# Layer 1 of an MLP by Strassen's scheme on blocks of 512 tokens, and square sums in the exponential's bias

## The chip, the cores and the metric

The kernel runs on one core of a Trainium2 chip, as one launch with one instruction list for each engine: PE (TensorE), ACT (ScalarE), DVE (VectorE), POOL (GpSimd) and SP (SyncE, which issues all DMAs). The metric is the device time of one execution in microseconds.

## The reference

```python
# attention, batch 8, 8 heads, 576 tokens, head size 64, 128 random features
scale = 1 / sqrt(sqrt(64))
def phi(x):
    proj = x @ omega.T                          # 128 features
    sq = sum(x * x, axis=-1) / 2
    h = proj - sq
    return exp(h - max(h)) / sqrt(128)
q_p, k_p = phi(q * scale), phi(k * scale)
num = q_p @ (k_p.T @ v);  den = q_p @ sum(k_p) + 1e-6
x = num / den                                   # 4608 tokens x 512
# MLP, w_in 512 x 2048, w_out 2048 x 512
h = x @ w_in
g = where(h > 0, h, exp(min(h, 0)) - 1)
out = g @ w_out
```

The weights come in float64. They are converted on the chip, from their 64-bit words.

## The kernel before

**Precision.** A matmul of the MLP is made of three passes in fp32r, high x high, high x low and low x high. Each operand is split into a rounded high part (a cast) and a low part (a subtraction).

**Attention.** A pair is two heads of one batch entry; there are 32 pairs, four to a batch. `load_pair`, `project` (k and q), `kv` and `finish` emit a pair's work. Of the first pairs (7 for k, 8 for q, `NNAT`) the projection runs natively in fp32, with the squares as extra rows of the matmul. For the others x is split into high and low in one tile (`tk`, `tq`), a matmul of 256 columns gives two parts in PSUM (`pp`), ACT copies the second part with the square sum as its bias and a scale of -1 (`rest`, line 497, one instruction per 128 rows), DVE subtracts it and takes the maximum (line 506), ACT negates the maximum (`negate`, line 410), and ACT takes the exponential (line 404). `finish` divides, transposes and multiplies; its result goes as high and low parts into rings of two batches of tokens, `xh` and `xl`.

**MLP.** Twelve blocks of 384 tokens, 16 steps each; a step is one 128-column slice f of w_in and the same rows of w_out. `layer1` makes 4 x 3 matmuls of 384 columns into a PSUM bank `ph` (two of them in turn, lines 764 to 766). The tile goes through ACT (Relu of -h, Exp, lines 773 and 774), DVE (line 777, which reads `e` in SBUF and `ph` in PSUM), a cast to the high part of `g` (line 333) and a subtraction for its low part (line 336, POOL or DVE). `layer2` makes 3 x 3 matmuls of 512 columns into three banks `acc` (lines 798 to 800).

**Weights.** `from_f64` converts a 128 x 512 chunk: two ACT passes, then on DVE a clamp (697, sometimes POOL), a shift (704) and a merge (709), then an integer addition on POOL (712), a cast to the high part, a subtraction to the low part on POOL (336). There are 32 chunks, 16 of each matrix. w_out stays in SBUF (`w2h`, `w2l`). w_in goes to a scratch buffer `w1s` in DRAM and is fetched again, 512 KB a step, into `w1c` (three buffers). Blocks 0 to 2 run in halves: first slices 0 to 7 of blocks 0, 1 and 2, then slices 8 to 15, with the first halves' sums parked in DRAM (`part`). A slice is converted ahead of its step of block 0, so the second eight are due while blocks 1 and 2 run their first halves.

**Order.** Nothing is scheduled on the chip. `Plan` takes each operation with an engine, a cost in ns, a due time, reads and writes, plays them through a model of engines, buffers and latencies, and writes each engine's list in the order it finds. Some operations name a second engine (`alt`, table `ALT`). On the chip each engine runs its list in order and waits on semaphores. Batch 0 comes ahead of the MLP, batch 1 beside block 0, and batches 2 to 7 beside blocks 2, 3, 5, 6, 8 and 9.

## Time and profile before

| | |
|---|---|
| three runs | 1092.15, 1090.98, 1088.34 us; median 1090.98 |
| profiled execution, span of its instructions | 1090.7 us (no other time of that execution is listed) |
| busy, share of the span | PE 97%, PEld 86%, ACT 66%, DVE 58%, POOL 37% |
| chain that ended last | PE 79%, DVE 9%, ACT 6%, issue 3% |
| layer 1 matmuls (764 to 766), busy | 787.0 us in 2304, modelled ends that overlap |
| layer 2 matmuls (798 to 800), busy | 686.5 us in 1728 |
| HBM | 155.48 MB read, 20.19 MB written |

How to read it: a matmul's record runs to a modelled end, so records overlap and a group's busy time is more than its share of the span; the distance from start to start is what a matmul costs in a stream. The granted clock of PE is given as a share of full speed. On DVE, ACT and POOL a record runs to the acknowledged write. A record's length includes time in which the engine holds the instruction and can't go on.

### The profile page before, as it was taken

How to read it: one execution, taken by the hardware profiler on the slowest of the kernel's cores; microseconds unless marked ns; L12 is line 12 of the kernel's file. 1: busy time of each engine (PE TensorE's matmuls, PEld its weight loads, DVE VectorE, ACT ScalarE, POOL GpSimd, SP SyncE). 2: the span in 40 equal slices, each digit the busy share in tenths (PEclk: the TensorE clock that was granted, in tenths of full speed). 3: DMA queues.
4: the chain of work that ended last, by engine and by line, in shares of the span. 5: the costliest groups of instructions: out<-in, count | busy, mean ns of one | idle time of the engine just before them, and what ended most of it. 6: DMA issues, size and time to landing. Idle time of an engine off the chain costs nothing.

```text
span 1090.7 us, 19072 instructions
## 1 busy us (share of the span) xinstructions
PE 1060.6 (97%) x5971; PEld 936.8 (86%) x5971; DVE 635.9 (58%) x2403; ACT 724.7 (66%) x2027; POOL 404.4 (37%) x372
## 2 busy tenths in 40 slices
...
GB/s 213 171 181 161 208 188 240 218 186 205 207 205 130 169 170 150 165 118 157 176 155 153 193 139 170 162 119 150 162 155 167 157 164 79 117 164 119 161 121 63
DMA packets 53235, 176.90 MB, mean 162 GB/s; under 512 B 6032, under 2 KB 6224, under 8 KB 53136
## 3 DMA queue, kind: packets, MB, share of 16 engines
...
q14 instruction: 51, 0.42, 0.1%
HBM read 155.48 MB, written 20.19 MB: 161 GB/s over the span
## 4 chain that ended last, share of the span: by engine, by line
PE 79%; DVE 9%; ACT 6%; issue 3%; DMA 1%; POOL 1%; SPq 0%; DVEq 0%; POOLq 0%; ACTq 0%
PE ph L764 11%; PE acc L798 10%; PE acc L800 10%; PE ph L766 10%; PE acc L799 10%; PE ph L765 10%; PE pkv L535 4%; PE ppq L488 3%; PE pn L634 3%; PE pt L607 2%; PE ppk L488 2%; ACT hk L404 1%; DVE u_w L697 1%; DVE u_w L704 1%; DVE u_w L709 1%
## 5 line engine op out<-in xcount | busy, mean ns | idle before, releaser
L336 POOL TENSOR_TENSOR g<-e,g 128x384 fp32r<-128x384 f32 x182 | 189.2, 1040 | 547.7 <-DVE g L333 405.9
L764 PE MATMUL ph<-xh,w1c 128*128 128x384 f32 x768 | 267.5, 348 | 6.7 <-DVE e L777 6.2
L766 PE MATMUL ph<-xh,w1c 128*128 128x384 f32 x768 | 259.8, 338 | 0.0
L765 PE MATMUL ph<-xl,w1c 128*128 128x384 f32 x768 | 259.7, 338 | 0.0
L777 DVE SCALAR_TENSOR_TENSOR e<-e,ph 128x384 f32<-128x384 f32 x192 | 105.9, 552 | 237.2 <-ACT e L774 232.8
L798 PE MATMUL acc<-w2h,g 128*128 128x512 f32 x576 | 231.4, 402 | 0.0
L773 ACT ACTIVATE e<-ph 128x384 f32<-128x384 f32 x192 | 93.6, 488 | 206.4 <-PE ph L766 198.4
L800 PE MATMUL acc<-w2h,g 128*128 128x512 f32 x576 | 227.7, 395 | 0.0
L799 PE MATMUL acc<-w2l,g 128*128 128x512 f32 x576 | 227.4, 395 | 0.0
L764 PEld LDWEIGHTS ph<-xh,w1c 128*128 128x128 f32 x768 | 145.6, 190 | 20.1 <-DVE e L777 8.5
L765 PEld LDWEIGHTS ph<-xl,w1c 128*128 128x128 f32 x768 | 145.8, 190 | 7.2
L766 PEld LDWEIGHTS ph<-xh,w1c 128*128 128x128 f32 x768 | 145.4, 189 | 0.3 <-POOL w1c L336 0.3
L800 PEld LDWEIGHTS acc<-w2h,g 128*128 128x128 f32 x576 | 108.5, 188 | 25.5
L798 PEld LDWEIGHTS acc<-w2h,g 128*128 128x128 f32 x576 | 108.7, 189 | 15.1 <-issue 2.3
L799 PEld LDWEIGHTS acc<-w2l,g 128*128 128x128 f32 x576 | 108.8, 189 | 12.2
L336 POOL TENSOR_TENSOR hq<-hq,den 128x512 f32<-128x512 f32 (+1 forms) x96 | 90.4, 961 | 36.1 <-DVE den L595 24.6
L774 ACT ACTIVATE e<-e 128x384 f32<-128x384 f32 x192 | 100.7, 525 | 3.1
L333 DVE CAST g<-e 128x384 fp32r<-128x384 f32 x166 | 72.8, 439 | 23.5 <-PE acc L800 18.8
L586 DVE CUSTOM_DVE_ANT_0 junk<-hq,pz 128x128 f32<-128x128 f32 (+1 forms) x320 | 74.1, 279 | 16.9 <-PE pz L570 16.1
L506 DVE CUSTOM_DVE_ANT_0 hq<-ppq,p2q 128x128 f32<-128x128 f32 x216 | 54.3, 287 | 41.8 <-ACT p2q L497 40.2
L506 DVE CUSTOM_DVE_ANT_0 hk<-ppk,p2k 128x128 f32<-128x128 f32 x225 | 56.5, 286 | 36.1 <-ACT p2k L497 34.3
L497 ACT ACTIVATE p2q<-ppq,sqq 128x128 f32<-128x128 f32 x216 | 67.8, 367 | 12.5 <-PE ppq L488 10.8
...
## 6 DMA issues: line engine op xcount, KB each, us to landing
w1c<-w1s SPq DMA_DIRECT2D x176, 512.0 KB, 3.3
...
```

Source lines behind the costliest of these rows:

```text
L336: (nc.vector if e == "DVE" else nc.gpsimd).tensor_tensor(*args)
L506: nc.vector.tensor_tensor_reduce(out=h()[:, j, :], in0=view()[:, a, 0:M], in1=p2()[:, a, :], scale=1.0, scalar=LOWEST, op0=ALU.subtract, o ...
L586: nc.vector.tensor_tensor_reduce(out=junk()[r], in0=h()[r, j, :], in1=pz()[r, a * P:(a + 1) * P], scale=1.0, scalar=EPS, op0=ALU.mult, op1 ...
L764: nc.tensor.matmul(ph(), wh, xh[:, c, o:o + TB], start=(c == 0), stop=False)
L765: nc.tensor.matmul(ph(), wh, xl[:, c, o:o + TB], start=False, stop=False)
L766: nc.tensor.matmul(ph(), wl, xh[:, c, o:o + TB], start=False, stop=(c == NC - 1))
L773: op("ACT", act(TB, True), due, lambda: nc.scalar.activation(e(), ph(), AF.Relu, scale=-1.0), (p,), (e,))
L774: op("ACT", act(TB), due + 0.2, lambda: nc.scalar.activation(e(), e(), AF.Exp, scale=-1.0), (e,), (e,))
L777: lambda: nc.vector.scalar_tensor_tensor(e(), e(), -1.0, ph(), ALU.add, ALU.max), (p, e), (e,),
L798: nc.tensor.matmul(a(), g()[:, 0, ts], w2h[:, f], start=(f == f0), stop=False)
L799: nc.tensor.matmul(a(), g()[:, 0, ts], w2l[:, f], start=False, stop=False)
L800: nc.tensor.matmul(a(), g()[:, 1, ts], w2h[:, f], start=False, stop=(f == f1 - 1))
```

## The change

Layer 1 now takes nine blocks of 512 tokens and pairs of slices (8 steps j a block, e = 0 or 1 in a pair). Features (two halves), tokens (two halves T of 256) and slices (two) form 2 x 2 blocks, and one level of Strassen's scheme in Winograd's form gives the four results from seven products of half size: a product is 2 x 3 matmuls of 256 columns. The x sides (`units`: x11, x21, x22 and four sums, split into high and low, `xo`) are made once a block, the weight sides (`convert`: four sums, seven pieces `w1p`, split) once in block 0, written to `w1s` and fetched in each later block, 256 KB a piece. Products 0, 5, 6 and 3 add up in one bank A, with a copy to SBUF between them (`save`); products 1, 4 and 2 go to one bank B, from which DVE forms three of the four results in SBUF (`total`, `h`). So `e` is now made from `h` in SBUF for three tiles of four. Halved blocks and `part` are gone: all weights are converted within block 0. Batch s+1 of attention runs beside block s, s = 0 to 6. PSUM: four banks `acc`, A, B, and two shared ones `pa` (before: three `acc`, two `ph`, three `pa`). Attention's result is kept once, unsplit, in `xs`. In the projection, the second part is copied without bias, 256 columns at a time, DVE adds instead of subtracting, and the square sum goes into the exponential's bias by two small DVE operations (`bias`) instead of `rest` and `negate`. The model's price of a matmul changes from n/2.4 + 2.5 to n/2.2 + 1 ns.

```diff
-TB = 384
-NTT = TB // P
-NBLK = NTOK // TB
+SB = 512
+TH = SB // 2
+NTT = SB // P
+NSB = NTOK // SB
+NJP = NF // 2
+NPROD = 7
...
+NLARGE = 6
+NPIECE, NUNIT, NU, NXT, NRAW, NHS, NG = 7, 7, 3, 3, 3, 4, 5
+
+
+MLP0 = 56.0
+STEP0, STEP_ATT, STEP = 16.0, 13.3, 10.8
...
-SPLIT = (0, 8, 16)
-NHALF = 3
...
+ORDER = (0, 1, 5, 4, 6, 3, 2)
+L1_AT = {0: 0.0, 1: 0.08, 5: 0.2, 4: 0.28, 6: 0.36, 3: 0.52, 2: 0.6}
+LAG2 = 0.75
...
-    w1s = dram.tile([NF, P, 2 * NC * P], F32, name="w1s")
-    part = dram.tile([3 * TB, DM], F32, name="part")
-    xh = const.tile([P, NC, RING], F32R, name="xh")
-    xl = const.tile([P, NC, RING], F32R, name="xl")
+    w1s = dram.tile([NJP * NPROD, P, 4 * P], F32, name="w1s")
+    xs = const.tile([P, NC, RING], F32, name="xs")
...
+        return Buf(ps, [P, 512], F32, tag, name, dict(pa=2).get(tag, 1))
...
+        def bias(g, js, due):
+            def f():
+                nc.vector.scalar_tensor_tensor(mx()[:, js], mx()[:, js], SCALE, sq()[:, js], ALU.mult, ALU.subtract)
+                nc.vector.scalar_tensor_tensor(nb()[:, js], mx()[:, js], -1.0, sq()[:, js], ALU.mult, ALU.subtract)
+
+            op("DVE", 2 * dve(4), due, f, ((mx, g), sq), ((mx, g), (nb, g)))
+
+        y = large([P, 2 * S], F32R, f"t{nm}_{i}")
...
-            def rest(c=c, n=n, p2=p2, view=view):
-                for a in range(n):
-                    j = 2 * c + a
-                    nc.scalar.activation(
-                        p2()[:, a], view()[:, a, M:], AF.Identity, bias=sq()[:, j:j + 1], scale=-1.0
-                    )
-
-            op("ACT", n * act(M, True, True), d + 0.5, rest, (p, sq), (p2,))
+            op(
+                "ACT", act(n * M, True), d + 0.5,
+                lambda e, n=n, p2=p2, view=view: copy(e, p2()[:, 0:n], view()[:, 0:n, M:]), (p,), (p2,),
+                alt=other("part", "DVE", dve(n * M)),
+            )
 
             def ttr(c=c, n=n, p2=p2, view=view):
                 for a in range(n):
                     j = 2 * c + a
                     nc.vector.tensor_tensor_reduce(
                         out=h()[:, j, :], in0=view()[:, a, 0:M], in1=p2()[:, a, :], scale=1.0, scalar=LOWEST,
-                        op0=ALU.subtract, op1=ALU.max, accum_out=mx()[:, j:j + 1],
+                        op0=ALU.add, op1=ALU.max, accum_out=mx()[:, j:j + 1],
...
+            o = qs.start + (b % 2) * S
+            op(
+                "ACT", act(n, True), d + 0.8 + half, lambda e, o=o, n=n, p=p: copy(e, xs[:, hp, o:o + n], p()[:, 0:n]),
+                (p,), [("xs", hp, z) for z in range(o // D, (o + n) // D)], alt=other("xs", "DVE", dve(n)),
...
+    def convert(j, due):
+
+        u = [from_f64(w1[2 * j + e], f"w1_{2 * j + e}", due) for e in range(2)]
+
+        def block(e, half):
+            return lambda: u[e]()[:, half * 2 * P:(half + 1) * 2 * P]
+
+        a11, a12, a21, a22 = (block(e, half) for e in range(2) for half in range(2))
+        sums = [Buf(sb, [P, TH], F32, "hs", f"sw_{j}_{e}", NHS) for e in range(4)]
+        s1, s2, s3, s4 = sums
+        add(2 * P, s1, a21, a22, ALU.add, (u[1],), (s1,), due - 4, "conv_add")
+        add(2 * P, s3, a11, a21, ALU.subtract, (u[0], u[1]), (s3,), due - 4, "conv_add")
+        add(2 * P, s2, s1, a11, ALU.subtract, (s1, u[0]), (s2,), due - 3.9, "conv_add")
+        add(2 * P, s4, a12, s2, ALU.subtract, (u[0], s2), (s4,), due - 3.8, "conv_add")
+        made = {0: (a11, (u[0],)), 1: (a12, (u[0],)), 5: (s2, (s2,)), 4: (s1, (s1,)), 6: (s3, (s3,)), 3: (a22, (u[1],)), 2: (s4, (s4,))}
+        for n, p in enumerate(ORDER):
+            t = piece(0, j, p)
+            src, reads = made[p]
+            split(2 * P, src, lambda t=t: t()[:, 0], lambda t=t: t()[:, 1], reads, (t,), due - 3.5 + 0.3 * n)
+            op(
+                "SP", 500, due, lambda t=t, p=p: nc.sync.dma_start(w1s[j * NPROD + p], flat(t)),
+                ((t, "h"), (t, "l")), (("w1s", j, p),), P * 2048,
+            )
+        for e in range(2):
+            f = 2 * j + e
+            v = from_f64(w2[f], f"w2_{f}", due + CONV2 + 2 * e)
+            split(512, v, lambda f=f: w2h[:, f], lambda f=f: w2l[:, f], (v,), ("w2", f), due + CONV2 + 2 * e - 4)
...
...
+        def unit(p, src, due):
+            t = xu[s, p] = Buf(sb, [P, 2, 2, TH], F32R, "xo", f"xo_{s}_{p}", NUNIT)
+            for d, n in cuts:
+                hi, lo = (lambda d=d, n=n, z=z: t()[:, z, :, d:d + n] for z in range(2))
+                op(
+                    "DVE", dve(2 * n, True), due, lambda e, d=d, n=n, hi=hi: copy(e, hi(), src[0](d, n)),
+                    src[1](d, n), ((t, "h", d),), alt=other("unit", "ACT", act(2 * n)),
+                )
+                op(
+                    "POOL", pool(2 * n), due + 0.4,
+                    lambda e, d=d, n=n, hi=hi, lo=lo: tt(e, lo(), src[0](d, n), hi().bitcast(F32), ALU.subtract),
+                    (*src[1](d, n), (t, "h", d)), ((t, "l", d),), alt=other("unit", "DVE", dve(2 * n)),
...
+        x11, x12, x21, x22 = (x(half, T) for half in range(2) for T in range(2))
+        unit(0, x11, due)
+        unit(1, x21, due + 0.5)
+        t3 = binary("t3", x22, x12, ALU.subtract, due + 0.8)
+        t2 = binary("t2", t3, x11, ALU.add, due + 0.9)
+        unit(5, t2, due + 1.0)
+        t1 = binary("t1", x12, x11, ALU.subtract, due + 1.3)
+        unit(4, t1, due + 1.5)
+        unit(6, t3, due + 2.0)
+        t4 = binary("t4", x21, t2, ALU.subtract, due + 2.3)
+        unit(3, t4, due + 2.5)
+        unit(2, x22, due + 3.0)
...
+        A = Buf(ps, [P, 512], F32, "pA", f"A_{s}_{j}", 1)
+        B = Buf(ps, [P, 512], F32, "pB", f"B_{s}_{j}", 1)
...
+        def product(p, bank, first):
+            w, x = w1p.pop((s, j, p)), xu[s, p]
+
+            def mms():
+                o = bank()[:, 0:TH]
+                for i in range(2):
+                    wh, wl = (w()[:, z, i * P:(i + 1) * P] for z in range(2))
+                    h, l = (x()[:, z, i] for z in range(2))
+                    for n, (a, b) in enumerate(((wh, h), (wh, l), (wl, h))):
+                        nc.tensor.matmul(
+                            o, a, b, start=(first and i == 0 and n == 0), stop=(i == 1 and n == 2),
+                            skip_group_check=True,
+                        )
+
+            op("PE", mm(TH, 6), due + st * L1_AT[p], mms, ((w, "h"), (w, "l"), *xu[s, p, "keys"]), (bank,))
...
+        def save(nm, at):
+            t = Buf(sb, [P, TH], F32, "cp", f"{nm}_{s}_{j}", 3)
+            op(
+                "ACT", act(TH, True), due + st * at, lambda e: copy(e, t(), A()[:, 0:TH]), (A,), (t,),
+                alt=other("part", "DVE", dve(TH)),
+            )
+            return t
+
+        def total(e, T, t, at):
+            h = Buf(sb, [P, TH], F32, "hs", f"h_{s}_{j}_{e}{T}", NHS)
+            op(
+                "DVE", dve(TH), due + st * at,
+                lambda: nc.vector.tensor_tensor(h(), B()[:, 0:TH], t(), ALU.add), (B, t), (h,),
+            )
+            elu(e, T, lambda: h(), h, False, at + 0.05)
...
+            y = Buf(sb, [P, TH], F32, "e", f"e_{s}_{j}_{e}{T}", 3)
+            g = gt[s, j, e, T] = Buf(sb, [P, 2, TH], F32R, "g", f"g_{s}_{j}_{e}{T}", NG)
+            op("ACT", act(TH, psum), d, lambda: nc.scalar.activation(y(), src(), AF.Relu, scale=-1.0), (key,), (y,))
+            op("ACT", act(TH), d + 0.2, lambda: nc.scalar.activation(y(), y(), AF.Exp, scale=-1.0), (y,), (y,))
+            op(
+                "DVE", dve(TH), d + 0.6,
+                lambda: nc.vector.scalar_tensor_tensor(y(), y(), -1.0, src(), ALU.add, ALU.max), (y, key), (y,),
...
+        product(0, A, True)
+        product(1, B, True)
+        c1 = save("c1", 0.1)
+        total(0, 0, c1, 0.18)
+        product(5, A, False)
+        product(4, B, True)
+        c2 = save("c2", 0.3)
+        product(6, A, False)
+        c3 = save("c3", 0.45)
+        total(1, 1, c3, 0.48)
+        product(3, A, False)
+        product(2, B, False)
+        elu(1, 0, lambda: A()[:, 0:TH], A, True, 0.62)
+        total(0, 1, c2, 0.7)
...
+    for s in range(NSB):
+        pace = (begin[s + 1] - begin[s]) / NJP
+        units(s, begin[s] - 3.0)
+        if s + 1 < B:
+            t0, t1 = begin[s], begin[s + 1] - TAIL_B
+            for hp in range(NHP):
+                pair((s + 1) * NHP + hp, t0 + (t1 - t0) * (hp + 1) / NHP)
+        for j in range(NJP):
+            if s:
+                fetch(s, j, step(s, j))
+            else:
+                convert(j, step(0, j) - CONV1)
+            layer1(s, j, step(s, j), pace)
+            layer2(s, j, step(s, j), pace)
+
```

The lists show the change in two places. First POOL's, in the middle of the conversion in block 0, before. `w1c` and `w2l` are low parts of weights, `u_w` the integer addition, `hq` the division in attention:

```order
L336 TENSOR_TENSOR w2l<-u_w_4_1052,w2h 128x512
L336 TENSOR_TENSOR w1c_1203<-u_w_6_1090,w1c_1203 128x512
L712 TENSOR_TENSOR u_w_5_1156<-u_w_5_1156,raw_w_5_1102 128x512
L336 TENSOR_TENSOR w2l<-u_w_5_1156,w2h 128x512
L712 TENSOR_TENSOR u_w_7_1292<-u_w_7_1292,raw_w_7_1173 128x512
L336 TENSOR_TENSOR w1c_1361<-u_w_7_1292,w1c_1361 128x512
```

And after, slices 10 and 11, `w1p_5_*` being the pieces of step 5:

```order
L692 TENSOR_TENSOR u_w_10_1690<-u_w_10_1690,raw_w_10_1571 128x512
L323 TENSOR_TENSOR g_3_01_1798<-e_3_01_1759,g_3_01_1798 128x256
L692 TENSOR_TENSOR u_w_11_1740<-u_w_11_1740,raw_w_11_1628 128x512
L323 TENSOR_TENSOR w1p_5_0_1809<-u_w_10_1690,w1p_5_0_1809 128x256
L323 TENSOR_TENSOR w1p_5_1_1814<-u_w_10_1690,w1p_5_1_1814 128x256
L323 TENSOR_TENSOR w1p_5_5_1862<-sw_1_1850,w1p_5_5_1862 128x256
L692 TENSOR_TENSOR u_w_10_1825<-u_w_10_1825,raw_w_10_1731 128x512
L323 TENSOR_TENSOR w1p_5_4_1884<-sw_0_1838,w1p_5_4_1884 128x256
L323 TENSOR_TENSOR w2l<-u_w_10_1825,w2h 128x512
L692 TENSOR_TENSOR u_w_11_1871<-u_w_11_1871,raw_w_11_1811 128x512
```

One low part of 512 columns per slice has become seven of 256 per pair of slices, and they stand between the g tiles of the step that runs. DVE's list beside it has four sums (`sw`) and casts of 256 columns in the same place.

Second PE's, in the last block, where no attention runs. Before:

```order
L800 MATMUL acc_0_2_11968<-w2h,g_12194 128x512
L764 MATMUL ph_12281<-xh,w1c_12209 128x384
L765 MATMUL ph_12281<-xl,w1c_12209 128x384
L766 MATMUL ph_12281<-xh,w1c_12209 128x384
```

After (A, B and `acc` are banks, `xo` units, `w1p` pieces; the number after the step is the product):

```order
L825 MATMUL A_5_15063<-xo_0_14308,w1p_5_0_14948 128x256 x6
L825 MATMUL B_5_15070<-xo_1_14320,w1p_5_1_14964 128x256 x6
L897 MATMUL acc_3_14592<-w2h,g_4_11_15032 128x512
L898 MATMUL acc_3_14592<-w2l,g_4_11_15032 128x512
L899 MATMUL acc_3_14592<-w2h,g_4_11_15032 128x512
L825 MATMUL A_5_15063<-xo_5_14337,w1p_5_5_14978 128x256 x6
L897 MATMUL acc_0_14549<-w2h,g_4_10_15049 128x512
L898 MATMUL acc_0_14549<-w2l,g_4_10_15049 128x512
L899 MATMUL acc_0_14549<-w2h,g_4_10_15049 128x512
L825 MATMUL B_5_15070<-xo_4_14360,w1p_5_4_14998 128x256 x6
```

Before, a slice's twelve matmuls stood together and layer 2's nine after them. Now a product's six alternate with groups of three matmuls of layer 2 of the step before, and the next product on the same bank comes one or two groups later.

272 lines of the change are left out of this document (109 added, 163 removed).

## The prediction

> **What bounds the kernel now.** I read the page first, then a table of stretches, then the matmul stream in order of time.
>
> ```profile
> span 1090.7 us, 19072 instructions
> PE 1060.6 (97%) x5971; PEld 936.8 (86%) x5971; DVE 635.9 (58%) x2403; ACT 724.7 (66%) x2027; POOL 404.4 (37%) x372
> ```
>
> PE is busy 97%. The sum below is made against this execution's 1090.7 us, 0.3 below the median of the three runs (1090.98); anything under 0.3% (3.3 us) can't be told from no change.
>
> ```profile
> 0.00:55.00 55.00, 47.50 (x312) 42.02 (x313) 39.75 (x131) 41.38 (x133) 25.68 (x28) 0.88 0.64 193
> 55.00:137.00 82.00, 71.80 (x447) 58.59 (x446) 72.02 (x210) 65.51 (x190) 60.06 (x47) 0.96 0.56 183
> 137.00:183.00 46.00, 40.11 (x195) 34.91 (x193) 41.29 (x89) 31.24 (x73) 26.78 (x20) 0.93 0.61 210
> 183.00:214.00 31.00, 30.21 (x154) 27.09 (x154) 22.69 (x35) 13.69 (x26) 18.69 (x16) 1.00 0.61 216
> 214.00:250.00 36.00, 35.37 (x175) 30.96 (x174) 25.98 (x35) 15.42 (x30) 22.89 (x18) 1.00 0.58 207
> 439.00:508.00 69.00, 69.00 (x366) 62.98 (x365) 21.21 (x66) 28.54 (x71) 16.71 (x16) 1.00 0.43 149
> 508.00:604.00 96.00, 95.82 (x565) 84.22 (x564) 63.43 (x301) 82.25 (x244) 32.24 (x31) 1.00 0.49 160
> 604.00:694.00 90.00, 90.00 (x525) 79.29 (x524) 57.48 (x266) 73.03 (x213) 29.88 (x30) 1.00 0.49 160
> 1014.00:1091.00 77.00, 73.02 (x363) 64.97 (x361) 14.97 (x33) 19.55 (x38) 17.20 (x17) 1.00 0.32 112
> ```
>
> Columns: length, busy PE, PEld, DVE, ACT, POOL, granted clock, DMA share, GB/s. From 183 on PE never rests; before that it does, and at 55 to 183 DVE and POOL are busy 113 and 87 of 128 us. There are two regimes, and the change touches both.
>
> **Regime 1, PE-bound: what seven products save.**
>
> ```profile
> 1055.52 0.34 PE L764 MATMUL ph<-xh,w1c 128*128 128x384 f32 x1
> ...
> 1057.60 0.39 PE L798 MATMUL acc<-w2h,g 128*128 128x512 f32 x1
> ...
> 1059.69 0.34 PE L764 MATMUL ph<-xh,w1c 128*128 128x384 f32 x1
> ```
> ```profile
> 603.62 0.52 PE L488 MATMUL ppq<-om,tq 128*128 128x256 f32 x3
> 603.97 0.33 PE L764 MATMUL ph<-xh,w1c 128*128 128x384 f32 x1
> ```
>
> Ends overlap, so starts count. Twelve matmuls of 384 columns take 1057.60-1055.52 = 2.08 us (0.173 each), nine of 512 take 2.09 (0.232): a step is 4.17 us. Three of 256 columns, the form that layer 1 gets, take 0.35 (0.117). Layer 1 has 12x16x4x3 = 2304 matmuls now and 9x8x7x2x3 = 3024 then: 399.4 against 353.8 us. **Saved on PE: 45 us.** Layer 2 stays at 1728 of 512, attention's matmuls stay.
>
> A rival here is a fixed cost per matmul, which more and smaller ones would multiply. The Trainium skill (TensorE: Matmul & The Clock Gate, section Back-to-back issue gap) gives sustained 81 ns at 128 columns and 131 ns at 512; by my interpolation that is 114 at 384 and 98 at 256, layer 1 would go from 263 to 295 us, and the forecast would rise by 78. From rows: 0.232-0.173 = 0.059 per 128 columns leaves nothing fixed at 384 (3x0.059 = 0.177), and the three at 0.117 lie on that line. If 5 ns were fixed, 720 more matmuls cost 4 us. The page's figures do not hold for this stream.
>
> **Regime 2, the weight conversion: two engines that take turns.**
>
> ```profile
> 107.70 1.29 POOL L336 TENSOR_TENSOR w1c<-u_w,w1c 128x512 fp32r<-128x512 f32 x1
> ...
> 108.11 1.11 DVE L333 CAST g<-e 128x384 fp32r<-128x384 f32 x1
> ...
> 1055.72 0.36 DVE L333 CAST g<-e 128x384 fp32r<-128x384 f32 x1 [0.33 <-PE acc L800]
> ```
>
> The same cast takes 0.36 us when POOL is idle; begun beside a POOL operation it ends 0.22 us after that one. The next rows give minimum/median/maximum ns of the operations of both engines. DVE's stretch by up to 1.2 us, with one exception, L777, which has an input in PSUM:
>
> ```profile
> L712 POOL TENSOR_TENSOR u_w<-u_w,raw_w x32: 1279/1310/1841, 16.5 to 238.4; 128x512 int32<-128x512 int32 x32
> L709 DVE SCALAR_TENSOR_TENSOR u_w<-raw_w,u_w x32: 677/692/1676, 15.6 to 237.7; 128x512 int32<-128x512 int32 x32
> L704 DVE TENSOR_SCALAR u_w<-u_w x32: 410/426/1529, 15.2 to 236.1; 128x512 int32<-128x512 int32 x32
> L697 DVE TENSOR_SCALAR u_w<-u_w x27: 412/702/1543, 13.4 to 232.8; 128x512 f32<-128x512 f32 x27
> L697 POOL TENSOR_SCALAR u_w<-u_w x5: 1906/1917/2093, 88.6 to 234.1; 128x512 f32<-128x512 f32 x5
> L336 POOL TENSOR_TENSOR w2l<-u_w,w2h x16: 1267/1473/1832, 36.8 to 187.0; 128x512 fp32r<-128x512 f32 x16
> L336 POOL TENSOR_TENSOR w1c<-u_w,w1c x16: 1282/1304/1627, 22.0 to 242.1; 128x512 fp32r<-128x512 f32 x16
> L333 DVE CAST w1c<-u_w x13: 416/515/1523, 29.8 to 240.4; 128x512 fp32r<-128x512 f32 x13
> L336 POOL TENSOR_TENSOR hq<-hq,den x96: 392/1040/1562, 23.2 to 942.0; 128x512 f32<-128x512 f32 x64, 128x128 f32<-128x128 f32 x32
> L336 POOL TENSOR_TENSOR g<-e,g x182: 992/1012/1519, 80.6 to 1081.3; 128x384 fp32r<-128x384 f32 x182
> L333 DVE CAST g<-e x166: 328/360/1456, 83.2 to 1080.8; 128x384 fp32r<-128x384 f32 x166
> L336 DVE TENSOR_TENSOR g<-e,g x10: 543/550/1650, 83.9 to 239.9; 128x384 fp32r<-128x384 f32 x10
> L336 DVE TENSOR_TENSOR tk<-xk,tk x41: 751/1084/1725, 94.6 to 898.0; 64x576 fp32r<-64x576 f32 x41
> L777 DVE SCALAR_TENSOR_TENSOR e<-e,ph x192: 535/554/556, 79.4 to 1079.9; 128x384 f32<-128x384 f32 x192
> ```
>
> So POOL's work and DVE's work on SBUF alone (casts, scalar steps, two SBUF inputs) add up on one shared resource; call it the port. I sum it at the minima. Up to 250 us, where the conversion has ended: POOL 32x1.28 + 16x1.27 + 16x1.28 + 5x1.91 + hq 12x1.04 and 8x0.39 + 21 g at 0.99 + 7 attention operations on 64 partitions at some 1.3 = 137; DVE 27x0.41 + 32x0.41 + 32x0.68 + 25 weight casts at 0.42 + 22 g casts at 0.33 + 10x0.54 + 7 of tk's kind at 0.75 = 74. Together 211 of the 238 us since 12: 89%. At 55 to 183 alone it is 121 of 128, 95%: there the port is the bound and PE waits. The last part of the conversion hides: from 183 to 250 PE has blocks 1 and 2 to work on and is busy 65.6 of 67.
>
> **What the change adds to the port.** All conversion must now end inside block 0, since each step's seven pieces are made just ahead of its products, and every engine runs its list in order. Counting the order's rows up to block 0's last g tile, with 256-column prices between the rows above (POOL 0.69, midway between 0.39 at 128 and 0.99 at 384; DVE cast 0.24, two inputs 0.41, both on the lines through 384 and 512): POOL 32x1.28 + 16x1.27 + 55 piece lows at 0.69 + 7x1.91 + 19 for hq + 24 g at 0.69 + 4x1.27 unit lows + 1 = 154. DVE 25x0.41 + 32x0.41 + 32x0.68 + 30 sums at 0.41 + 53 piece casts at 0.24 + 16x0.42 + 24 STTs, now with h in SBUF instead of PSUM, at 0.41 + 19x0.24 + 8x0.41 + 6x0.75 + units 8 = 107. Together **262 us**, with only block 0 and batch 1 for PE to do. From 12 us on that ends at 274 if the port never rests, 288 at 95%, 306 at 89%. I take 288, the rate of the stretch where the port was the bound. SP's list costs there too: the 56 writes of w1s (16 before) wait for POOL's lows, and loads of raw weights stand behind them, three raw buffers deep; that is why I do not take 100%. Below nothing (a gain) only if the two engines could overlap, which the maxima exclude except at edges.
>
> **The rest, PE-bound again.** 439 to 694 is three blocks of 16 steps and two batches of attention: 255 - 48x4.17 = 54.8, so 27.4 us a batch with its stalls. A new block: 8x(42x0.117+24x0.232) = 83.9. Six blocks with a batch and two without: 6x111.3+2x83.9 = 836. The order lets PE do some 10 us of block 1 and batch 2 before block 0 ends (-10), and after PE's last matmul come 4 us (77-73).
>
> New waits: A and B are one bank each, so PE waits for ACT's copy or DVE's sum between products.
>
> ```profile
> 1053.25 0.34 PE L766 MATMUL ph<-xh,w1c 128*128 128x384 f32 x1
> ...
> 1053.68 0.49 ACT L773 ACTIVATE e<-ph 128x384 f32<-128x384 f32 x1 [3.13 <-PE ph L766]
> ...
> 1054.83 0.55 DVE L777 SCALAR_TENSOR_TENSOR e<-e,ph 128x384 f32<-128x384 f32 x1 [2.93 <-ACT e L774]
> ```
> ```profile
> L331 ACT CAST xh<-pn 128x256 fp32r<-128x256 f32 x32 | 11.9, 373 | 8.0 <-PE pn L634 8.0
> L497 ACT ACTIVATE p2k<-ppk,sqk 128x128 f32<-128x128 f32 x225 | 68.3, 364 | 8.1 <-PE ppk L488 7.2 <-DVE mxk L506 0.7
> ```
>
> Last matmul to ACT's start is 0.43, a 256-column copy 0.37, back some 0.1: 0.9 us from start to start, 0.8 beside the matmul itself. The order keeps two layer-2 groups (2x3x0.232 = 1.4) there in clean blocks: hidden. With attention ACT is 86% busy (82.25 of 96), so copies queue. Queued behind such a wait on PE is layer 2 of the step before. Zero to 45 us over eight blocks; I take 15, nearer the low end because attention blocks lose little today (508 to 604: PE idle 0.2). If the cover goes, each late copy costs PE its whole queue time.
>
> Off the path: the 441 L497 passes (160 us of ACT) become 245 copies (196x0.37 + 49 short ones, about 86), 98 negations on ACT become 196 tiny DVE operations; 216 saves (80 us) land on ACT, 216 totals (about 90) on DVE. ACT and DVE stay below PE's share in blocks with attention, so I cost this at nothing, bounds -5 to +15 (in the 15 above). The 448 fetches of 256 KB against 176 of 512 KB are hidden: a piece's buffer is refilled a whole step, 10 us, ahead. The units of a block (eleven operations and seven lows) run under the last step of the block before; what stays is in the 15 too. Part's DMAs vanish at no gain.
>
> **Sum.** 288 + 836 - 10 + 4 + 15 = **1133 us**. That is 42 above the 1091 of before: the 45 saved on PE come back nearly twice as idle time of PE in block 0.
>
> **Rivals.** (a) The port gives way: POOL and DVE overlap better than the maxima show, block 0 goes at PE's pace. PE has block 0's 84 us to do by then, two batches at some 33 each (27.4, and the native projections of the first pairs cost more) and the 10 us ahead, 160 in all; before, the first 250 us hold 25 us of idle PE and about 11 lost to a granted clock of 0.88 to 0.96. Block 0 would end at 196 and the rest takes 845: 1041, **faster**. The other side begins where block 0 ends before 242 (1087-845), 32 us earlier than a port that never rests allows. Against it: 95% at 55 to 183. 0.09. (b) Bank waits take more than 45 us: 1165 to 1210. For it: seven waits on ACT or DVE among a step's products where layer 1 had one, and DVE's sums now stand behind operations that wait for POOL. Against it: 0.8 us needed, 1.4 given. 0.13. (c) A fixed cost of 5 to 15 ns a matmul, 1137 to 1144: 0.02. (d) The port partly eased, block 0 ending near 245, about 1090: no change. 0.05. (e) My forecast, 1100 to 1165: 0.71.
>
> **How the numbers follow.** Faster 0.09 and the upper edge of (d): 0.10; same 0.05; slower 0.85. The range 1100 to 1170 leaves out (a), (d) and most of (b).
>
> **What would show it.** First product of block 1 at 275 to 305 us, PE busy 50 to 60% at 60 to 280, casts and scalar steps on DVE with maxima over 1.2 us, granted clock dips there; from 300 on PE at 97% or more, attention blocks of 111 to 116 us, clean ones of 84 to 86; matmuls of 256 columns 0.117 apart. Wrong if block 0 ends near 200, or if PE idles behind L825 on ACT's copies in every step.

## The result, and the profile after

The changed kernel takes 1159.8 us (median of 4 runs, 1156.5 to 1161.7) against 1090.7 for the kernel before on the same chip: ratio 1.064, 95% interval 1.062 to 1.066, 69 us slower. The forecast was 1133, range 1100 to 1170, slower with 0.85.

The page of the profiled execution (its span, the engines' busy time and three rows of tenths in 40 slices):

```profile
span 1157.7 us, 22479 instructions
PE 1063.4 (92%) x6691; PEld 910.2 (79%) x6691; DVE 874.3 (76%) x3121; ACT 779.3 (67%) x2180; POOL 500.9 (43%) x552
PE   7867777778999899989999999999989999999998
DVE  7999999989677877777778777877797667546443
PEclk9869998898999999999999999999989999999999
```

PE fell from 97% to 92%. DVE is at 90% and more in slices 2 to 8, where the weights are converted, and the granted clock has its lowest tenths there (6 in slice 3, 8 in 2, 7 and 8).

The table of stretches, cut at the first product of a block (columns as in the prediction). First block 0, then blocks 1 to 6 together, then single blocks: 2, 5, 6 with attention, 7 and 8 without:

```profile
54.40:259.40 205.00, 152.17 (x841) 120.19 (x841) 197.36 (x461) 116.70 (x316) 147.22 (x135) 0.88 0.52 166
259.40:975.50 716.10, 692.59 (x4480) 598.24 (x4479) 542.37 (x2329) 544.25 (x1539) 263.31 (x314) 0.99 0.56 180
384.90:504.30 119.40, 115.75 (x750) 99.83 (x749) 89.89 (x394) 92.74 (x262) 44.63 (x55) 0.99 0.57 184
740.80:864.40 123.60, 115.33 (x749) 99.64 (x748) 97.74 (x406) 91.98 (x262) 50.07 (x62) 0.98 0.56 180
864.40:975.50 111.10, 110.20 (x716) 95.97 (x715) 76.85 (x348) 80.09 (x229) 37.89 (x45) 0.99 0.54 166
975.50:1064.20 88.70, 85.86 (x531) 76.06 (x530) 51.01 (x108) 37.58 (x96) 32.31 (x36) 1.00 0.57 179
1064.20:1157.70 93.50, 89.32 (x546) 79.19 (x546) 37.92 (x92) 39.47 (x97) 26.08 (x34) 1.00 0.53 161
```

Block 0 ends at 259.4, 29 us earlier than the 288 of the sum, and still takes 205 us. Everything behind it takes 898.3 us where the forecast had 845. By the prediction's rows of before, the same later work (4096 tokens and six batches) took 10.67 x 66.7 + 6 x 27.4 + 4 = 880 us there. So of the 67 us between the two profiled executions some 49 are lost in block 0 (259 against 1091-880 = 211), and 18 behind it: the saving on PE shows nowhere as time.

The matmul stream in a clean block (one without attention), in order of time:

```profile
1013.66 0.88 PE L825 MATMUL A<-xo,w1p 128*128 128x256 f32 x6
1014.38 0.40 PE L897 MATMUL acc<-w2h,g 128*128 128x512 f32 x1
1014.62 0.40 PE L898 MATMUL acc<-w2l,g 128*128 128x512 f32 x1
1014.86 0.39 PE L899 MATMUL acc<-w2h,g 128*128 128x512 f32 x1
1015.09 0.39 PE L897 MATMUL acc<-w2h,g 128*128 128x512 f32 x1
```

Six matmuls of 256 columns take 0.72 us from start to start, 0.120 each (forecast 0.117), three of 512 take 0.71, 0.237 each; the median over the run is 0.234.

The groups of operations behind the sum on the port (minimum/median/maximum ns; the first, second, fifth and sixth within block 0, the others over the run):

```profile
L320 DVE CAST w1p<-sw x28: 276/288/1378, 76.4 to 239.9; 128x256 fp32r<-128x256 f32 x28
L320 DVE CAST w1p<-u_w x21: 279/283/1400, 58.0 to 239.0; 128x256 fp32r<-128x256 f32 x21
L844 DVE TENSOR_TENSOR h<-B,c x216: 387/424/427, 80.8 to 1147.2; 128x256 f32<-128x256 f32 x108
L856 DVE SCALAR_TENSOR_TENSOR e<-e,A x72: 403/416/424, 89.0 to 1147.6; 128x256 f32<-128x256 f32 x72
L323 POOL TENSOR_TENSOR w1p<-sw,w1p x28: 724/855/1244, 76.7 to 240.8; 128x256 fp32r<-128x256 f32 x28
L692 POOL TENSOR_TENSOR u_w<-u_w,raw_w x27: 1269/1408/1828, 55.7 to 233.5; 128x512 int32<-128x512 int32 x27
L856 DVE SCALAR_TENSOR_TENSOR e<-e,h x216: 393/426/1534, 82.6 to 1148.7; 128x256 f32<-128x256 f32 x108
```

The reading of the port holds. Over 288 operations with an input in PSUM (B or A) the longest takes 0.427 us. The same SCALAR_TENSOR_TENSOR (STT) with both inputs in SBUF goes up to 1.53, and casts of 0.28 up to 1.40. In order of time, a stretch of block 0:

```profile
76.73 0.84 POOL L323 TENSOR_TENSOR w1p<-sw,w1p 128x256 fp32r<-128x256 f32 x1 [1.17 <-DVE w1p L320]
76.91 0.94 DVE L320 CAST xo<-xs 128x512 fp32r<-128x512 f32 x1
...
77.53 1.44 POOL L323 TENSOR_TENSOR xo<-xt_t,xo 128x512 fp32r<-128x512 f32 x1
77.77 1.34 DVE L320 CAST w1p<-sw 128x256 fp32r<-128x256 f32 x1
```

POOL's first operation ends at 77.57, DVE's cast at 77.85, POOL's next at 78.97, DVE's next at 79.11. Each begins beside the other engine's operation and ends after it: the cast of 256 columns 0.14 us after it, where alone it takes 0.28, the cast of 512 columns 0.28 after it, where alone it takes 0.41. So at such a change of turn, in either direction, some 0.13 us of the later operation's shortest record are hidden behind the earlier one (median 0.125 over the 219 changes of turn in block 0).

What PE waited for (us in all, times, longest), in block 0 and then in blocks 1 to 5:

```profile
PE B L825 <- DVE h L844: 16.3, 9, 3.1
PE acc L899 <- DVE g L323: 4.0, 3, 2.0
PE ppk L485 <- DVE mxk L500: 3.7, 3, 2.3
...
PE ppq L485 <- DVE z L320: 6.7, 5, 4.7
PE B L825 <- DVE h L844: 6.2, 7, 1.8
PE ppq L485 <- DVE mxq L500: 4.4, 6, 1.5
```

DVE is named in the longest of these rows. The view leaves out short gaps, and so does the busy share (692.6 of 716.1 us in blocks 1 to 6), since the records reach over them: a matmul of 256 columns is recorded at 0.28 us and costs 0.12. Counted over all pairs of consecutive matmuls, as distance beyond the usual one of the form (0.119, 0.233 and for attention's forms about 0.11), PE loses 90 us in block 0, 65 in blocks 1 to 6 (some 420 gaps of 0.15 us), 3.6 in block 7 and nothing in block 8. Before, a batch of attention lost about 3.5 by the same count.

### The profile page after: what moved, and what is told of

Read it like the earlier page. It is cut to its first block, busy times and chain, and to the rows that moved or that the text cites. A ratio compares the mean times of both kernels' runs of the same rounds, so it can differ in the third digit from the quotient of the medians.

```text
span 1157.7 us, 22479 instructions
## 1 busy us (share of the span) xinstructions
PE 1063.4 (92%) x6691; PEld 910.2 (79%) x6691; DVE 874.3 (76%) x3121; ACT 779.3 (67%) x2180; POOL 500.9 (43%) x552
## 4 chain that ended last, share of the span: by engine, by line
PE 53%; DVE 28%; ACT 7%; DMA 5%; issue 4%; POOL 1%; SPq 0%; DVEq 0%; ACTq 0%; POOLq 0%
PE A L825 12%; PE B L825 9%; PE acc L897 7%; PE acc L898 7%; PE acc L899 7%; DVE e L856 4%; PE pkv L529 3%; DVE junk L580 2%; PE ppq L485 2%; PE pt L601 2%; DVE xo L320 2%; DVE xt_t L323 2%; PE pn L628 2%; DVE w1p L320 2%; DVE u_w L689 1%
## 5 line engine op out<-in xcount | busy, mean ns | idle before, releaser
L323 POOL TENSOR_TENSOR g<-e,g 128x256 fp32r<-128x256 f32 x276 | 215.1, 781 | 524.0 <-DVE g L320 374.0
L825 PE MATMUL A<-xo,w1p 128*128 128x256 f32 x1728 | 263.9, 289 | 11.4 <-DVE e L856 4.5
L825 PEld LDWEIGHTS A<-xo,w1p 128*128 128x128 f32 x1728 | 239.7, 193 | 37.6 <-ACT c L318 7.7
L825 PE MATMUL B<-xo,w1p 128*128 128x256 f32 x1296 | 201.8, 293 | 25.2 <-DVE h L844 24.6
L825 PEld LDWEIGHTS B<-xo,w1p 128*128 128x128 f32 x1296 | 177.7, 194 | 48.9 <-DVE h L844 36.1
L856 DVE SCALAR_TENSOR_TENSOR e<-e,h 128x256 f32<-128x256 f32 x216 | 122.8, 568 | 94.5 <-ACT e L853 92.7
L852 ACT ACTIVATE e<-h 128x256 f32<-128x256 f32 x216 | 90.5, 419 | 109.6 <-DVE h L844 91.8
L844 DVE TENSOR_TENSOR h<-B,c 128x256 f32<-128x256 f32 x216 | 90.6, 419 | 73.4 <-PE B L825 35.8
L318 ACT COPY c<-A 128x256 f32<-128x256 f32 x216 | 79.8, 369 | 80.7 <-PE A L825 78.5
L853 ACT ACTIVATE e<-e 128x256 f32<-128x256 f32 x288 | 119.8, 419 | 4.7
```

The lines of the kernel that those rows point to most:

```text
L323: (nc.vector if e == "DVE" else nc.gpsimd).tensor_tensor(*args)
L825: nc.tensor.matmul(o, a, b, start=(first and i == 0 and n == 0), stop=(i == 1 and n == 2), skip_group_check=True,)
L844: lambda: nc.vector.tensor_tensor(h(), B()[:, 0:TH], t(), ALU.add), (B, t), (h,),
L852: op("ACT", act(TH, psum), d, lambda: nc.scalar.activation(y(), src(), AF.Relu, scale=-1.0), (key,), (y,))
L853: op("ACT", act(TH), d + 0.2, lambda: nc.scalar.activation(y(), y(), AF.Exp, scale=-1.0), (y,), (y,))
L856: lambda: nc.vector.scalar_tensor_tensor(y(), y(), -1.0, src(), ALU.add, ALU.max), (y, key), (y,),
```

## The experiments

Each run was timed in three rounds against the kernel before. From its trace stand the lengths of block 0 and of blocks 1 to 6, and the prediction's sum made again: every POOL operation, and every DVE operation on SBUF alone, that begins in block 0, at the shortest duration of its form in that trace (without DVE's accumulator reads, row sums, reciprocals and the `bias` operations, some 10 us in the changed kernel). PE's waits in blocks 1 to 6 are given where they were counted.

The expectations name their theories by letters. P: the port bounds block 0. D: DVE's list bounds it, whatever POOL does. D2: DVE's own work bounds it, together with the time that it is held up behind POOL. S: SP's list, the raw buffers or the transfers. C: a chain through all engines. K: too few banks. A: ACT is late.

| kernel | median us | ratio to before | block 0 | sum on the port | blocks 1 to 6 | PE's waits there |
|---|---|---|---|---|---|---|
| changed | 1159.8 | 1.064 (1.062 to 1.066) | 205.0 | 227 | 716.1 | 65 |
| weight lows on DVE | 1151.9 | 1.057 (1.052 to 1.061) | 198.1 | 221 | 713.6 | |
| weight lows as copies on ACT | 1141.1 | 1.045 (1.041 to 1.049) | 190.4 | 186 | 715.9 | |
| weight casts on ACT | 1151.8 | 1.055 (1.053 to 1.058) | 198.7 | 215 | 716.9 | |
| no weight lows | 1129.0 | 1.034 (1.032 to 1.035) | 174.9 | 184 | 713.8 | 63 |
| integer addition off POOL | 1137.2 | 1.042 (1.040 to 1.044) | 188.4 | 202 | 716.2 | 65 |
| no g lows | 1137.3 | 1.043 (1.040 to 1.046) | 200.2 | 213 | 699.1 | 50 |
| third shared bank | 1162.9 | 1.065 (1.063 to 1.067) | 206.9 | 234 | 716.1 | 69 |
| second bank B | 1170.0 | 1.072 (1.070 to 1.073) | 208.0 | 228 | 724.3 | 74 |
| no denominators | 1154.8 | 1.058 (1.056 to 1.060) | 205.6 | 232 | 711.1 | 62 |
| no Relu | 1157.0 | 1.059 (1.056 to 1.063) | 208.6 | 235 | 712.4 | 64 |
| changed, bias undone | 1174.0 | 1.075 (1.072 to 1.078) | 199.4 | 225 | 736.2 | 84 |
| before, bias alone | 1096.6 | 1.005 (1.003 to 1.006) | | | | |

### Block 0: is it the port?

**Weight lows on DVE.**

```diff
-            "POOL", pool(n), due + 0.5, ... alt=other("conv_sub", "DVE", dve(n)),
+            "DVE", dve(n), due + 0.5, ...
```

> The changed kernel with the low parts of the weights (pieces and w_out) always on DVE, none on POOL. Theory P (POOL and DVE take turns on one port, and the port bounds block 0): a low part holds the port shorter on DVE (0.41 against 0.72 us at 256 columns, 0.68 against 1.26 at 512), 55 x 0.31 + 16 x 0.58 = 26 us less; at a hold of 95% block 0 ends 28 us earlier, at 232 instead of 259, time about 1132. Theory D (DVE's own list bounds block 0, POOL is beside it): DVE gets 55 x 0.41 + 16 x 0.68 = 33 us more, block 0 ends near 292, time about 1192. Theory S (SP's list, the raw buffers or the transfers bound it): block 0 stays at 255 to 265, time 1155 to 1165.

Block 0 in this run's table of stretches:

```profile
54.70:252.80 198.10, 151.40 (x835) 121.41 (x833) 191.25 (x495) 119.91 (x321) 115.59 (x91) 0.85 0.52 170
```

DVE has 34 operations more, POOL 44 fewer, and the block is 7 us shorter, not longer. So DVE's own work is not the bound by itself. The time, 1151.9, lies between theory P's 1132 and theory S's 1155. The 28 us of theory P did not come: of 52 us taken off POOL the planner filled half with other work, and the sum on the port fell by 6, not 26.

**Weight lows as copies on ACT, and no weight lows.**

```diff
-            "POOL", pool(n), due + 0.5, lambda e: tt(e, lo(), src(), hi()..., ALU.subtract), ...
+            "ACT", act(n), due + 0.5, lambda: nc.scalar.copy(lo(), src()), ...
```
```diff
-            "POOL", pool(n), due + 0.5, lambda e: tt(e, lo(), src(), hi()..., ALU.subtract), ...
-    nc.sync.dma_start(w1s[j * NPROD + p], flat(t))
+    nc.sync.dma_start(w1s[...] as (p, 2, c), t()[:, 0:1] twice)
```

> The changed kernel with the low parts of the weights written by a plain copy on ACT (the subtraction is left out, the low part is not the difference). It takes 55 x 0.72 + 16 x 1.26 = 60 us off POOL and the port, and adds 55 x 0.39 + 16 x 0.55 = 30 us to ACT, which is 57% busy in block 0. Theory P: block 0 ends up to 63 us earlier, at 196 to 215 (PE's own work ends near 196), time 1097 to 1115. Theory D: DVE's list is as it was, block 0 stays at 255 to 262, time about 1158. Theory S: the same, 1155 to 1165.

> The changed kernel with the 72 low parts of the weights left out and nothing in their place (the high part is written to the scratch buffer twice and multiplied twice, so DMA bytes and PE's work are the same). Takes 60 us off POOL and the port and adds nothing to any engine, where the copies on ACT added 30 us to ACT. Theory P with ACT as the second bound (ACT ate the rest of that run's gain): block 0 ends at 205 to 220, time 1105 to 1120. Theory C (no single resource: each step of block 0 is a chain through ACT, DVE, POOL and PE held by the buffers, and taking one engine's load away moves little): block 0 ends at 235 to 242 as with the copies on ACT, time 1135 to 1143.

Block 0 of the first, then of the second:

```profile
50.10:240.50 190.40, 150.44 (x834) 120.70 (x833) 171.41 (x460) 137.63 (x378) 97.81 (x84) 0.86 0.56 184
```
```profile
53.90:228.80 174.90, 143.93 (x836) 116.09 (x834) 165.22 (x440) 112.61 (x306) 96.61 (x82) 0.89 0.61 191
```

The sum on the port falls by 41 and 43 us, the block by 15 and by 30. With the same POOL work the run without the 25 us on ACT has a block 0 that is 15 us shorter (12 us of time, since it begins 4 us later). That points to ACT as the next bound, but it isn't shown: in this run the products of block 0 also wait for the high part alone, and no run separates the two. DVE's busy time fell by 26 and 32 us though it lost 1 and 21 operations of 461: what it lost is mostly time spent waiting inside a record. Theories D and S fall with both runs. Theory P in the strict form (every us off the port is a us of time) falls too. Both times lie between what the theories gave: 1141 for the first (P 1097 to 1115, D 1158), 1129 for the second (P 1105 to 1120, C 1135 to 1143).

**Weight casts on ACT.**

```diff
-            "ACT", act(n), due, lambda e: copy(e, hi(), src()), ..., alt=other("conv_hi", "DVE", dve(n, True)),
+            "ACT", act(n), due, lambda: nc.scalar.copy(hi(), src()), ...
```

> The changed kernel with the casts of the weights (high parts of pieces and w_out) always on ACT. Takes 53 x 0.26 + 16 x 0.41 = 20 us off DVE and off the port, adds 53 x 0.39 + 16 x 0.55 = 29 us to ACT. Theory P and theory D: block 0 ends about 21 us earlier, near 238, time about 1138. Theory S, or a wait for ACT in the place of the one for DVE: no gain, 1155 to 1170.

Block 0 gains 6 us for 12 off the port, with 18 us more on ACT (134.8 against 116.7 busy): a third of the forecast by P. It begins 3 us earlier, and the time, 1151.8, lies between P's 1138 and the 1155 of no gain.

**Integer addition off POOL.**

```diff
-            nc.scalar.activation(low(), low().bitcast(U32), AF.Copy, scale=2.0 ** -29)
+            nc.scalar.activation(low(), low().bitcast(U32), AF.Copy, bias=-0.5, scale=2.0 ** -29)
-            nc.vector.tensor_scalar(ui(), ui(), 3, 0x7FFFFFFF, ALU.logical_shift_left, ALU.bitwise_and)
+            nc.vector.scalar_tensor_tensor(ui(), ui(), 3, low(), ALU.logical_shift_left, ALU.bitwise_or)
-        op("POOL", pool(512), due - 5, lambda: nc.gpsimd.tensor_tensor(ui(), ui(), low(), ALU.add), ...)
```

> The changed kernel with POOL's integer addition of the conversion (32 at 1.27 us or more) gone: ACT rounds the low word down, DVE's shift takes it in by a bitwise or (0.68 instead of 0.41 us), and the clamp stays on DVE (4 in block 0 were on POOL at 1.9). In block 0 POOL loses 27 x 1.27 + 4 x 1.9 = 42 us, DVE gets 27 x 0.27 + 4 x 0.41 = 9 us. Theory P: the port's sum falls by 33 us, block 0 ends 33 us earlier, time about 1127. Theory D2: DVE's own work rises by 9, its stretch (72 us beside 129 us of POOL, 0.56 us per us) falls by 23, block 0 is some 14 us shorter, time about 1146.

```profile
51.30:239.70 188.40, 150.37 (x843) 122.02 (x843) 180.43 (x460) 115.76 (x313) 118.16 (x114) 0.85 0.58 185
```

Time falls by 22 us, block 0 by 17, for 25 off the port (block 0 also begins 3 us earlier). That is between the two theories, 1127 and 1146. It is the best of the kernels that leave nothing out, 1.042 of the kernel before.

**Read together.** In eleven of the twelve kernels with Strassen's layer the sum on the port is 1.05 to 1.13 times block 0's length; the exception, 0.98, is the one with the copies on ACT. With what is hidden at the changes of turn taken off, the sum is 0.93 to 0.99 of block 0 in ten of them, and 0.87 and 0.91 in the two without POOL's weight lows: there something else begins to bound. The five runs in which the sum stayed within 2 us or rose did not shorten block 0 by more than 6 us: two with another bank (sum +7 and +1, block +2 and +3), one without denominators (+5 and +1), one without Relu, which takes 7 us off ACT there (+8 and +4), and the one with the bias undone (-2 and -6). A us off the port's sum was worth 0.35 to 0.7 us in five runs (and 7 for 6 with the lows on DVE). So the port is what block 0 mainly hangs on; ACT may come next. What stays open is DVE's part apart from the port (theory D2 against P): the run without denominators was to take 15 us of DVE's work on PSUM away, but the planner gave DVE other work in exchange. At shortest durations DVE's own work fell by 5 us only (154 to 149), and its busy time not at all (197.7), so the run does not tell.

### Blocks 1 to 6: where do 65 us of waits come from?

**No g lows.**

```diff
-            op("POOL", pool(TH), d + 1.2, lambda x: tt(x, g()[:, 1], y(), g()[:, 0]..., ALU.subtract), ...)
-                    nc.tensor.matmul(a(), g()[:, 1, ts], w2h[:, f], ...)
+                    nc.tensor.matmul(a(), g()[:, 0, ts], w2h[:, f], ...)
```

> The changed kernel without the low parts of g (the 288 subtractions, 276 of them on POOL at 0.78 us, are left out, and layer 2 multiplies the high part a second time in their place, so PE's work is the same). In block 0 this is 24 x 0.73 + 8 x 0.41 = 21 us less on the port. What it tells apart is the six later blocks with attention, where PE waits 65 us in all. Theory P (there too DVE's operations wait behind POOL's, and PE behind DVE): those waits fall to 20 to 30 us, blocks of 112 to 115 us, time about 1095 to 1105. Theory K (the banks: A, B and two shared ones instead of three set PE's waits): blocks 1 to 6 stay at 117 to 121 us in the mean, and only block 0 gains, time about 1137.

```profile
53.00:253.20 200.20, 155.49 (x861) 126.82 (x862) 190.89 (x455) 118.13 (x320) 134.28 (x117) 0.85 0.53 172
253.20:952.20 699.00, 679.46 (x4460) 590.67 (x4460) 525.35 (x2326) 538.50 (x1532) 115.22 (x122) 1.00 0.59 184
```

Blocks 1 to 6 lose 17 us and the waits fall from 65 to 50. POOL's 148 us less took 17 us off DVE's busy time with no operation fewer but three: port time again. The gaps fell ahead of `ppq` and B, by 11 us together, and by only 2 ahead of `acc`, where the link that was left out stood. The waits lie between the two theories, 20 to 30 and 65: a quarter of them is POOL's, three quarters are not. The time, 1137.3, is theory K's 1137 by chance, since block 0 gained 5 us where 21 were reckoned and the later blocks gained 17 where K had none.

**Third shared bank; second bank B.**

```diff
-                    acc[s, r] = Buf(ps, [P, DM], F32, f"acc{r}", ..., 1)
+                    acc[s, r] = acc[s, 2] if r == 3 else Buf(ps, [P, DM], F32, f"acc{r}", ..., 1)
-        dict(pa=2)
+        dict(pa=3)
```
```diff
-        B = Buf(ps, [P, 512], F32, "pB", f"B_{s}_{j}", 1)
+        B0 = Buf(ps, [P, 512], F32, "pB", f"B0_{s}_{j}", 2)
+        B = Buf(ps, [P, 512], F32, "pB", f"B_{s}_{j}", 2)
-        product(1, B, True)
+        product(1, B0, True)
```

> The changed kernel with three shared banks pa instead of two (as before the change). The bank comes from layer 2: token rows 2 and 3 are added into one bank acc, so the output is not the reference's, while the matmuls are as many. Theory K (too few banks): in the six later blocks with attention PE waits 28 of its 65 us ahead of ppq, ppk, pt and pn; most of that goes, and half of the 28 us ahead of the same in block 0: time 1120 to 1138. Theory P (DVE is late behind POOL, whatever the banks): 1150 to 1162.

> The changed kernel with two banks for B: product 1 goes to its own, products 4 and 2 to the other, so that product 4 need not wait for DVE's first sum. The bank comes from layer 2 as in the run with a third shared bank (rows 2 and 3 in one acc; the output is not the reference's). Theory K: PE waits 24.5 us ahead of B in block 0 and 17.6 us in blocks 1 to 6; about two thirds of it goes: time 1128 to 1140. Theory P: DVE's sums are as late as before and the next step waits for them instead: 1150 to 1162.

What PE waited for at A in blocks 1 to 5 (259 to 864 us) of the changed kernel; then blocks 1 to 6 and the same wait with a third shared bank, and again with a second bank B:

```profile
PE A L825 <- ACT c L318: 0.8, 1, 0.8
```
```profile
262.70:978.80 716.10, 685.85 (x4455) 592.24 (x4455) 547.80 (x2338) 532.36 (x1521) 253.38 (x302) 0.99 0.57 179
```
```profile
PE A L825 <- ACT c L318: 4.0, 8, 1.2
```
```profile
261.30:985.60 724.30, 692.68 (x4471) 596.71 (x4471) 548.52 (x2336) 540.67 (x1533) 265.69 (x314) 0.99 0.57 178
```
```profile
PE A L826 <- ACT c L318: 7.5, 7, 1.9
```

Theory K falls. A third shared bank took 28 us of gaps ahead of ppq, ppk, pt and pn to 22, a second B those ahead of B from 18 to 7, and both times the gaps ahead of A rose from 9 to 19. The wait moved to the next bank, and the time stayed or rose: 1162.9 and 1170.0, both above theory P's 1162. The bank taken from layer 2 is not what cost it, for the gaps ahead of `acc` in blocks 1 to 6 are 10 and 8 us against 10.

**No denominators; no Relu.**

```diff
             def dens(slots=slots, js=js):
+                if i >= NHP:
+                    nc.vector.tensor_copy(den()[:, js], pz()[:, js])
+                    return
```
```diff
-            op("ACT", act(TH, psum), d, lambda: nc.scalar.activation(y(), src(), AF.Relu, scale=-1.0), (key,), (y,))
-            op("ACT", act(TH), d + 0.2, lambda: nc.scalar.activation(y(), y(), AF.Exp, scale=-1.0), (y,), (y,))
+            op("ACT", act(TH, psum), d + 0.2, lambda: nc.scalar.activation(y(), src(), AF.Exp), (key,), (y,))
```

> The changed kernel without the denominators' products in attention (L580, ten DVE operations of 0.25 to 0.28 us and their accumulator reads a pair, which read hq in SBUF and pz in PSUM; left out for batches 1 to 7, a copy of a few columns of pz stands for den). This takes some 15 us off DVE in block 0 and 14 us a batch later, and nothing off POOL; since one input lies in PSUM, it takes nothing off the port either. Theory D2 (block 0 ends when DVE's list ends: its own 156 us and the stretch behind POOL; and in the later blocks PE waits for DVE because DVE is late): block 0 is 12 to 15 us shorter, at 190 to 193, the 65 us of waits in blocks 1 to 6 fall by 15 to 30, time 1115 to 1132. Theory P as the prediction had it (the sum on the port bounds): block 0 stays at 202 to 207, time 1150 to 1162.

> The changed kernel without the Relu passes (L852, 288 operations of ACT, 0.42 us from h and 0.38 from A; Exp reads h or A itself, so positive values come out as exp(h)-1). In blocks 1 to 6 this takes 144 x 0.42 + 48 x 0.38 = 79 us off ACT, as much as undoing the second part of the change put on it, and one operation out of each tile's chain; nothing off POOL, DVE or the port. Theory A (in the later blocks ACT is the engine whose lateness PE feels: 78 us more there cost 20 us, while 63 us less on DVE gave 5): blocks 1 to 6 fall from 716 to 690 to 700 us. Rival B (no engine: each late link is felt whatever engine it is on, and the list's order is fixed): 708 to 716. Block 0 by theory P (the port bounds it; ACT loses 13 us there): 202 to 207 us; if it falls by 10 or more, ACT's part in block 0 was underrated. Time 1133 to 1145 by A, 1148 to 1160 by the rival.

```profile
258.60:969.70 711.10, 686.12 (x4461) 593.66 (x4461) 512.54 (x1945) 530.08 (x1512) 264.01 (x307) 0.99 0.58 181
```
```profile
263.10:975.60 712.50, 683.80 (x4462) 588.62 (x4462) 542.50 (x2323) 481.87 (x1347) 268.74 (x312) 1.00 0.58 180
```

384 operations less on DVE (30 us of busy time) gain 5 us, 192 less on ACT (62 us of busy time) gain 4. Neither theory D2 nor theory A stands in these blocks: taking load off DVE or off ACT, each by itself, is not what ends PE's waits. The second run came out in the ranges of its rival (708 to 716 and 1148 to 1160), by which each late link is felt whatever engine it is on. Without denominators block 0 and the time are theory P's (202 to 207, 1150 to 1162); without Relu block 0 is 208.6, just above them.

### The second part of the change

**Bias alone on the kernel before; bias undone in the changed kernel.** The edit is the part of the change's diff from `bias` to `op0`, applied to the one and taken out of the other; in the second, p2 joins pa in the planner's list `LOOSE`.

> The kernel before with the second part of the change alone: the projection's second part is copied without bias, DVE adds, the square sum enters the exponential's bias. It frees some 74 us of ACT's list over the whole run and adds 126 small DVE operations pairs (some 0.35 us a pair). PE is the bound of that kernel, so the prediction's price of zero (bounds -5 to +15) gives 1086 to 1105, likeliest 1088 to 1093. A rival, that the freed ACT time lets PE run on where it idles before 183 us, would give 1078 to 1085.

> The changed kernel with layer 1 as changed and the second part of the change undone (ACT copies each 128 rows with the square sum as bias, DVE subtracts, ACT negates the maximum); in the planner p2 joins pa among the buffers taken out of turn. It takes some 31 us off DVE over the run and adds 51 us to ACT, as the run of the second part alone showed with signs turned. Theory D2: 1143 to 1153, the gain in block 0 and in blocks 1 to 6 alike. Rival A (ACT, 78% busy in blocks 1 to 6, becomes late in DVE's place): 1160 to 1175.

The stretch from 500 to 700 us, before and with the bias part alone; then blocks 1 to 6 with it undone:

```profile
500.00:700.00 200.00, 199.82 (x1170) 176.61 (x1170) 125.60 (x586) 161.30 (x473) 65.07 (x63) 1.00 0.48 158
```
```profile
500.00:700.00 200.00, 198.84 (x1163) 175.23 (x1162) 135.76 (x648) 147.43 (x387) 57.32 (x58) 1.00 0.49 160
```
```profile
255.70:991.90 736.20, 693.09 (x4489) 596.65 (x4488) 531.76 (x2161) 589.13 (x1806) 272.80 (x313) 0.99 0.56 176
```

On the kernel before the part costs 5 us (ratio 1.003 to 1.006): above the likeliest 1088 to 1093, inside 1086 to 1105. In the stretch shown 14 us go from ACT, 10 come to DVE, and PE, which rested 0.2 us there, now rests 1.2 in 200. In the changed kernel undoing it costs 14 us, all of it in blocks 1 to 6, where ACT gets 45 us more (block 0 gains 6, blocks 1 to 6 lose 20); 1174 lies in rival A's range. So 62 us of busy time off ACT gain 4, and 45 us on it cost 20 (by the sum of record lengths, 80 off and 92 on). The two kernels' orders differ in more than this part, so the size of the 14 is not the bias part's alone.

## Why the prediction came out as it did

The sign and the place of the largest loss were right: the port in block 0. That the time fell inside the range is in part luck, for two errors of opposite sign met: block 0 came 29 us earlier than the sum had it (alone, 1104), all that follows took 53 us longer (alone, 1186). Term by term:

- **45 us saved on PE**: 36 by the measured 0.120 (3024 x 0.120 = 363 against 399), and layer 2's 0.234 for 0.232 takes 3 back. 0.003 us a matmul was not seen in three matmuls of before. The rival of a fixed cost stays dead: the figures in the Trainium skill (TensorE: Matmul & The Clock Gate, section Back-to-back issue gap), 81 ns at 128 columns and 131 at 512, do not fit 0.120 at 256 and 0.234 at 512.
- **Block 0 at 288**: it ended at 259. The count was a little low (272 us by the trace from 12 us on, where I had 262); the failed step is the rate. I took the 95% of 55 to 183 in the kernel before for the ceiling of a sum of record lengths. It was none: the same sum over 55 to 137 of that kernel is already 82 of 82 us, and block 0 shows 110% (272 in 247 us). The part of each record that is hidden at a change of turn (0.13 us) must come off. The 219 changes of turn in block 0 take 32 us off its sum and leave some 196 of 205 us, 96%. The stretch of before has 84, which take 12 us off 122 and leave 110 of 128, 86%. So the rate came from a stretch that was not full, and with more and shorter operations the hidden part weighs more. The Trainium skill (Perfetto Trace Analysis, section DVE / Act Engine Instruction) says that a record ends with the write's acknowledgement; the trace agrees in so far as the sum exceeds the time. The Trainium skill (SBUF — State Buffer, section SBUF: two separate sides) says that GpSimd and DVE share a pair of ports under an exclusive lock, which DVE needs for two SBUF inputs or a two-port mode; the 288 operations with an input in PSUM that stay under 0.43 us agree with it.
- **836 for the eight later blocks, and 15 of new waits**: this is the term that failed most. From block 1 on it took 898.3 where 836 - 10 + 4 + 15 = 845 stood. Waits of 69 us stand where the sum had 15 and some 21 within the 27.4 a batch: 33 more. The matmuls' spacing is 11 (2688 x 0.003 + 1536 x 0.002). The rest of the 53, 9 us, is about the 10 of work ahead, of which block 1 shows nothing (111 us of work without its waits, where blocks 2 to 5 have 109). Block 0 even left work behind: 58 of its 64 groups of layer 2 were done when block 1 began.
- **"0.8 us needed, 1.4 given"**: true in clean blocks, 3.6 us of waits in block 7 and none in block 8. In blocks with attention PE waits ahead of every bank, some 420 times by 0.15 us. That each link (ACT's copy, DVE's sum, the STT) is late in its turn and uses up the cover is the reading that fits; it isn't shown link by link. The new waits came to 15 + 33 = 48, past the 45 at which rival (b) began; the time stayed below its 1165 only because block 0 took 29 less. Its mechanism was half right: in blocks 1 to 6 PE waits between the products too, but 27 of the 65 us lie ahead of A and B, the rest ahead of attention's banks and `acc`, and one more bank doesn't cure it.
- **Bias at nothing**: 5 us on the kernel before, within the bounds of -5 to +15.
- **What would show it**: DVE's maxima over 1.2 us, the clock's dips (0.88 in block 0) and PE near 97% from 300 on (831 of 858 us) came. Clean blocks of 88.7 instead of 84 to 86, attention blocks of 111 to 125 instead of 111 to 116, PE at 74% instead of 50 to 60 in block 0 did not. Neither sign of being wrong came: block 0 did not end near 200, and PE did not idle behind ACT's copies in every step.

What stays open is what three quarters of the waits in blocks 1 to 6 hang on. One more bank, less load on DVE and less load on ACT did not cure them, each by itself; all at once was not tried. Two candidates were not tried either. The planner prices a STT of 256 columns at 69 + 256/0.96 = 336 ns and a copy from PSUM at 264, where the trace has 0.43 and 0.37 us, so each list is laid out for links that come sooner than they do. And attention's large tiles share six buffers `w`, where the kernel before has ten (two `ld`, two `t`, four `h`, two `qh`).

No version here beats the kernel before. The best that leaves nothing out, the one without POOL's integer addition, would need another 45 us. Behind block 0 alone, the changed kernel is 18 us slower than the old one on the same work. So a cheaper conversion brings it back only if block 0 then ends more than 18 us ahead of the 211 of before; the earliest end here is 229, with the weight lows left out.
